# Attention of a fused three-stage kernel: one stay on TensorE per chunk in 64x64 shapes, q and v scaled ahead of the scores, a mask made on the chip, PSUM in pairs of banks, another order of loads

## The chip, the cores and the metric

The kernel runs on one core of a Trainium2 chip. Its five engines each work through a list of their own in order: TensorE (PE), VectorE (DVE), ScalarE (ACT), GpSimd (POOL), and SyncE (SP), which here only issues transfers. The metric is the device time of one execution in microseconds (us), lower is better.

## The reference, cut to what matters

```python
def _attn_ref(q, k, v):                      # 2 batches, 8 heads, 768 tokens, 64 wide
    gamma = 1.0 - 2.0 ** (-5.0 - np.arange(H))
    for t in range(S):
        state = gamma * state + np.einsum('bhd,bhe->bhde', k[:, :, t], v[:, :, t])
        y[:, :, t] = np.einsum('bhd,bhde->bhe', q[:, :, t], state) / np.sqrt(D)
...
def _moe_ref(x, w_in, w_out, alpha):         # x 1536 x 512, w_in 512 x 2048
    h = x @ w_in
    g = np.maximum(h, 0.0) + alpha * np.minimum(h, 0.0)
    return g @ w_out
...
def _moe2_ref(x, w_in, w_out, a, b):         # the same sizes
    h = x @ w_in
    P = a[0] + a[1] * h + a[2] * h**2 + a[3] * h**3
    Q = 1.0 + abs(b[0]) * np.abs(h) + abs(b[1]) * h**2
    g = P / (Q + 1e-06)
    return g @ w_out
```

Attention feeds the first feed-forward layer, and that feeds the second.

## The kernel before, in words

**Products.** A step i of `pe_h` (L334) computes a 128x512 piece of h for one of three token blocks b (512 tokens) and one of 16 blocks m of d_ff; `pe_out` (L351) adds that step's share to the four PSUM banks `acc`. Operands are split into a high and a low part (`xh`/`xl`, `wh`/`wl`, two halves of `g`), and three of the four cross products are kept, so that each of the two functions issues 12 matmuls of 128x128 by 128x512. There are 96 steps, 48 for each layer: 192 such groups of 12. A loop step i issues `pe_h(i + 2)`, then `pe_out(i)`.

**Weights.** They lie in memory as 64-bit numbers, 512 KB for each m and each of w_in and w_out. After the load (L270) a weight tile is decoded: abs on ACT (L278), three operations on DVE (L284, L288, L292; called words 0, 1 and 2 below), a cast on ACT (L303, the high part), a subtraction on DVE (L309, the low part). `START` says in which half step of the loop each of these is issued. A weight's number W0, W1, ... is its place in that order.

**The first layer's bend.** ACT makes two Relus of h (L369, L370, `act1_front`), DVE joins them (L375), ACT and DVE split the result into the parts of g (L380, L385).

**Attention.** Twelve chunks c of 128 tokens, six for each batch; four pairs j of heads, e is the head in its pair. For each chunk there are four loads of 256 KB (q and k transposed, k and v as they are), and TensorE computes the scores (L139), y from scores and v (L170), the growth of the state, called st (L182), and the share of y that comes from the state R (L193, the R part; none in chunks 0 and 6). DVE multiplies the scores by the decay table `dm` (L143, 512 KB, loaded once) and adds st to R (L205). For the R part a scaled q is made: four operations on ACT (L150) and one on POOL or DVE (L152); k is scaled for st on POOL (L123) or, in chunks 4 to 7, by eight operations on ACT (L120). In chunks 5 and 11 no st is needed. y goes to `xh` and `xl` (L212, L213). `att_b` issues the scores and the scaling of q, `att_c` all that follows.

**Order.** All instructions stand in the order in which the program writes them, on each engine. A start phase runs chunks 0 to 3 and decodes the first weight. A table then puts the rest of attention between the product groups, scores and y of a chunk at two places:

```python
stages = {-4: ("c", 4)}
for c, t, u in ((5, -3, -2), (6, -1, 1), (7, 2, 4), (8, 5, 6), (9, 7, 9), (10, 10, 12), (11, 13, 14)):
    stages[t] = ("b", c)
    stages[u] = ("c", c)
```

PSUM has eight banks: four hold `acc` (and, until the first `pe_out`, y), four go round in a ring for h, the scores and y. SP issues all loads in order; a load waits there until its tile is free.

## Time and profile before

| | us |
|---|---|
| median of 3 runs | 582.52 |
| lowest and highest run | 582.01, 582.68 |
| the profiled execution, its span | 582.5 |
| PE busy (matmuls) | 574.3 (99%) |
| DVE busy | 466.2 (80%) |
| ACT busy | 371.1 (64%) |
| POOL busy | 77.5 (13%) |

The span is the time of one profiled execution from its first to its last instruction; the times of runs are taken without the profiler. Matmuls are pipelined, so a busy PE isn't one at its peak: what a matmul takes is seen from where the next one starts.

### The profile page before, as it was taken

To read this page: it belongs to the slowest core of one execution; us is meant where nothing else is said; L and a number is where in the kernel's file an instruction comes from. 1 tells how busy PE (TensorE), PEld (TensorE's weight loads), DVE (VectorE), ACT (ScalarE), POOL (GpSimd) and SP (SyncE) were. 2 spreads that over 40 slices of the span, in tenths; PEclk is the share of its full clock that TensorE was granted. 3 is DMA by queue.
4 is the path that set the end of the run, shared out by engine and by line. 5 is a ranking of instruction groups with operands and counts; after the bars stand their busy time and mean duration, and the time that the engine had idled before them with its cause. 6 is when DMAs were issued, how large, how long until landed. Compare 5 with 4: busy or idle time off the path is not lost.

```text
span 582.5 us, 8124 instructions
## 1 busy us (share of the span) xinstructions
PE 574.3 (99%) x3040; PEld 473.3 (81%) x3040; DVE 466.2 (80%) x738; ACT 371.1 (64%) x679; POOL 77.5 (13%) x61
## 2 busy tenths in 40 slices
PE   8999999999999999999999999999999999999997
PEld 7878777888888888888888888888888888888885
DVE  1899688788684364548997999999998999887886
ACT  2687567656553453437765787777786786686672
POOL 1401100000000000000000312223222222221221
PEclk8999999999999999999999999999999999999999
DMA  8999422334321012112451011001111100010101
GB/s 298 335 379 378 160 73 73 112 106 145 108 73 36 1 37 73 37 37 96 171 203 37 1 37 36 19 19 37 37 37 37 37 0 1 0 73 2 53 19 74
DMA packets 18920, 50.78 MB, mean 87 GB/s; under 512 B 2624, under 2 KB 2752, under 8 KB 18880
## 3 DMA queue, kind: packets, MB, share of 16 engines
...
q8 instruction: 24, 0.39, 0.3%
...
## 4 chain that ended last, share of the span: by engine, by line
PE 87%; DMA 8%; DVE 2%; SPq 1%; ACT 1%; issue 0%
PE acc L351 43%; PE h L334 42%; DMA qk<-in_qT_dram 2%; DMA r<-in_w1i_dram 1%; DMA r<-in_w1o_dram 1%; DMA kv<-in_vn_dram 1%; DMA dq_sb<-in_dq_dram 1%; DMA kv<-in_kn_dram 1%; ACT qk L150 1%; PE y L170 1%; PE sc L139 1%; DVE p L448 0%; PE y L193 0%; SPq L103 0%; PE y L182 0%
## 5 line engine op out<-in xcount | busy, mean ns | idle before, releaser
L334 PE MATMUL h<-xh,wh 128*128 128x512 f32 x384 | 150.3, 391 | 0.0
L334 PE MATMUL h<-xl,wh 128*128 128x512 f32 x384 | 149.6, 389 | 0.0
L334 PE MATMUL h<-xh,wl 128*128 128x512 f32 x384 | 149.4, 389 | 0.0
L351 PE MATMUL acc<-wh,g 128*128 128x512 f32 x384 | 125.7, 390 | 0.0
L433 POOL TENSOR_TENSOR g<-as,g 128x512 fp32r<-128x512 f32 x47 | 64.6, 1374 | 446.9 <-PE acc L351 261.3
L351 PE MATMUL acc<-g,wh 128*128 128x512 f32 x384 | 118.9, 391 | 0.0
L334 PEld LDWEIGHTS h<-xh,wh 128*128 128x128 f32 x384 | 72.1, 188 | 15.7 <-issue 0.2
L351 PEld LDWEIGHTS acc<-wh,g 128*128 128x128 f32 x384 | 72.0, 188 | 15.6 <-DVE g L433 0.4
L334 PEld LDWEIGHTS h<-xl,wh 128*128 128x128 f32 x384 | 72.1, 188 | 15.0 <-DVE xl L213 0.2
L334 PEld LDWEIGHTS h<-xh,wl 128*128 128x128 f32 x384 | 72.0, 188 | 14.9
L351 PEld LDWEIGHTS acc<-g,wh 128*128 128x128 f32 x384 | 71.6, 188 | 15.5 <-issue 0.7
L303 ACT CAST wh<-z 128x512 fp32r<-128x512 f32 x64 | 39.6, 620 | 57.3 <-DVE z L292 57.3
L351 PE MATMUL acc<-g,wl 128*128 128x512 f32 x192 | 75.0, 391 | 0.7 <-DVE wl L309 0.6
L351 PE MATMUL acc<-wl,g 128*128 128x512 f32 x192 | 74.7, 389 | 0.0
L375 DVE SCALAR_TENSOR_TENSOR np<-np,nalpha_sb 128x512 f32<-128x512 f32 x48 | 36.0, 749 | 40.3 <-ACT np L370 40.3
L369 ACT ACTIVATE np<-h 128x512 f32<-128x512 f32 x48 | 28.5, 595 | 44.2 <-PE h L334 44.2
L396 ACT ACTIVATE as<-h 128x512 f32<-128x512 f32 x48 | 28.6, 596 | 41.3 <-PE h L334 41.3
L402 DVE SCALAR_TENSOR_TENSOR as<-as,bb_sb,rr 128x512 f32<-128x512 f32 x48 | 38.0, 791 | 13.1 <-ACT rr L397 13.1
L385 DVE TENSOR_TENSOR g<-np,g 128x512 fp32r<-128x512 f32 x48 | 33.2, 692 | 17.4 <-ACT g L380 17.2
L292 DVE SCALAR_TENSOR_TENSOR z<-r,z 128x512 uint32<-128x512 uint32 x64 | 44.9, 702 | 1.5
L288 DVE SCALAR_TENSOR_TENSOR z<-r,z 128x512 uint32<-128x512 uint32 x64 | 45.0, 702 | 1.0
L309 DVE TENSOR_TENSOR wl<-z,wh 128x512 fp32r<-128x512 f32 x64 | 45.0, 703 | 0.1
...
## 6 DMA issues: line engine op xcount, KB each, us to landing
...
```

Of the source, the lines that this page charges most:

```text
L288: nc.vector.scalar_tensor_tensor(out=zu, in0=lo, scalar=29, in1=zu, op0=ALU.logical_shift_right, op1=ALU.bitwise_or)
L292: nc.vector.scalar_tensor_tensor(out=zu, in0=hi, scalar=0x80000000, in1=zu, op0=ALU.bitwise_and, op1=ALU.bitwise_or)
L303: nc.scalar.copy(hi, Z[k])
L309: nc.vector.tensor_tensor(out=lo, in0=Z[k], in1=hi.bitcast(F32), op=ALU.subtract)
L334: nc.tensor.matmul(ps, w[:, ks], xs(hl, b, k, ALL), start=(n == 0), stop=(n == 11))
L351: nc.tensor.matmul(acc[0][k], a, c, start=(begin and n == 0), stop=(end != "" and n == 2))
L369: nc.scalar.activation(n, h, AF.Relu, scale=-1.0)
L375: nc.vector.scalar_tensor_tensor(out=p, in0=n, scalar=nalpha_sb[:, m:m + 1], in1=p, op0=ALU.mult, op1=ALU.add)
L385: nc.vector.tensor_tensor(out=gl, in0=p, in1=gh.bitcast(F32), op=ALU.subtract)
L396: nc.scalar.activation(s, h, AF.Square)
L402: nc.vector.scalar_tensor_tensor(out=s, in0=s, scalar=bb_sb[:, 1:2], in1=r, op0=ALU.mult, op1=ALU.add)
L433: eng.tensor_tensor(out=gl, in0=a, in1=gh.bitcast(F32), op=ALU.subtract)
```

## The change

- For each chunk from 4 on there is one place in the loop, the end of a step (`VISITS`), where `visit` issues the scores of the next chunk, then the R part, y and st of this one, then the mask, the state and x. Chunks 0 to 3 go through the same functions in the start phase.
- The scores are 16 matmuls with 64 rows, 64 columns and 128 moving columns, each half of the key tokens apart; the R part comes ahead of y. y and st of all chunks lie in one pair of banks. For pairs 2 and 3 the two heads' halves change places in x, and the load of w_in of the first layer changes the same halves of its rows (three transfers in place of one).
- q is scaled ahead of the scores (`att_q`, by one of six tables, on POOL; chunk 0 on DVE), v ahead of st and y (`att_v`, on ACT by eight operations, in chunks 0, 1 and 3 on POOL). ACT makes five of the tables from the one loaded (`att_table`, four operations each). k is not scaled. With this the scores need no decay: a 0/1 triangle made by POOL is multiplied on, one DVE operation of 128x1024 for a chunk. The load of `dm`, the second load of `dq` and the loads of k for chunks 5 and 11 go.
- PSUM is one tile of eight banks: 0 to 3 for `acc` (until the first `pe_out` also for attention), 4 and 5 for h, 6 and 7 for y and st. From the visit of chunk 6 on the next chunk's scores use banks 4 and 5 too. After the last visit h uses 6 and 7 as well.
- `act1_front` makes one Relu; the join reads h in PSUM, with 1 - alpha as its factor. It now stands ahead of the odd half step's decoding, not within it.
- `pe_h`, and `pe_out` where a sweep doesn't end, run pass by pass over the four k; `pe_out` takes wh, wl, wh against g's high, high and low half.
- The first weights are decoded one half step later, and the loads of the start phase stand in another order.

```diff
-    ring = ctx.enter_context(tc.tile_pool(name="ring", bufs=4, space=PSUM))
-    accp = ctx.enter_context(tc.tile_pool(name="accp", bufs=1, space=PSUM))
+    psp = ctx.enter_context(tc.tile_pool(name="psp", bufs=1, space=PSUM))
+    ps_all = psp.tile([P, 8 * 512], F32, name="ps")
...
+    def bank(k):
+        return ps_all[:, 512 * k:512 * k + 512]
+    def pair(k):
+        return ps_all[:, 1024 * k:1024 * k + 1024]
...
-    R = const.tile([P, NK, 64], F32, name="R")
-    dq_sb = one.tile([P, 512], F32, tag="dq", name="dq_sb")
-    dm_sb = alloc("dm_sb")
+    R = const.tile([P, NK * H64], F32, name="R")
+    mask = const.tile([P, P], F32, name="mask")
+    tabs = [alloc(f"dq{n}") for n in range(CPB // 2)]
+    dqt = [tabs[n // 2][:, 512 * (n % 2):512 * (n % 2) + 512] for n in range(CPB)]
...
+    def att_q(c, eng):
+        q = att[c]["q"]
+        eng.tensor_tensor(out=q, in0=q, in1=dqt[c % CPB], op=ALU.mult)
+    def att_v(c, eng):
+        v = r8(att[c]["v"])
+        o = 8 * (c % CPB)
+        if eng is nc.scalar:
+            for h in range(8):
+                nc.scalar.mul(v[:, h, :], v[:, h, :], cst_sb[:, o + h:o + h + 1])
+        else:
+            dk = cst_sb[:, o:o + 8].unsqueeze(2).to_broadcast([P, 8, H64])
+            eng.tensor_tensor(out=v, in0=v, in1=dk, op=ALU.mult)
+    def pe_sc(c, hp):
         a = att[c]
-        ps = [bank(f"sc{c}_{e}") for e in range(2)]
         for j in range(NK):
...
-            for j in range(NK):
-                js = slice(j * P, (j + 1) * P)
-                o = 8 * CPB + 4 * (c % CPB) + j
-                for ds, es in rows(c, j):
-                    nc.scalar.mul(a["qs"][ds, js], a["q"][es, js], cst_sb[es, o:o + 1])
-            eng = nc.gpsimd if c < 4 else nc.vector
-            eng.tensor_tensor(out=a["qs"], in0=a["qs"], in1=dq_sb, op=ALU.mult)
...
+            for n in range(2):
+                t0 = j * P + H64 * n
+                for e in range(2):
+                    o = 512 * e + j * P
+                    nc.tensor.matmul(
+                        hp[HALF[n], o:o + P], a["t"][HALF[e], t0:t0 + H64],
+                        a["q"][HALF[e], j * P:(j + 1) * P], start=True, stop=True,
+                    )
+    def att_mask(c, hp):
+        nc.vector.tensor_tensor(
+            out=r8(att[c]["s"]), in0=r8(hp), in1=mask.unsqueeze(1).to_broadcast([P, 8, P]), op=ALU.mult
+        )
...
+    def pe_y(c, vp, st):
+        a = att[c]
+        m = c % CPB
+        if m > 0:
+            for j, e in HEADS:
+                nc.tensor.matmul(
+                    yo(vp, j, e), R[HALF[e], H64 * j:H64 * j + H64],
+                    a["q"][HALF[e], j * P:(j + 1) * P], start=j % 2 == 0, stop=False,
+                )
+        for j, e in HEADS:
             h = 2 * j + e
             nc.tensor.matmul(
-                yo(j, e),
-                a["v"][:, 64 * h:64 * h + 64],
+                yo(vp, j, e), a["v"][:, H64 * h:H64 * h + H64],
                 a["s"][:, 512 * e + j * P:512 * e + (j + 1) * P],
-                start=j in starts,
-                stop=first and j == NK - 1,
+                start=m == 0 and j % 2 == 0, stop=not st and j % 2 == 1,
             )
...
+        if st:
+            pe_st(c, vp, True)
+    def pe_st(c, vp, joined):
+        a = att[c]
+        for j, e in HEADS:
+            hs = slice(H64 * (2 * j + e), H64 * (2 * j + e) + H64)
+            o = 512 * (j // 2) + 256 + H64 * (j % 2)
+            nc.tensor.matmul(
+                vp[HALF[e], o:o + H64], a["k"][:, hs], a["v"][:, hs],
+                start=not joined and j % 2 == 0, stop=j % 2 == 1,
+            )
...
+    def att_state(c, vp):
+        r, src = (t.rearrange("p (n f) -> p n f", n=2) for t in (R, vp))
+        src = src[:, :, 256:384]
+        if c % CPB == 0:
+            nc.scalar.copy(r, src)
+        else:
+            nc.vector.tensor_tensor(out=r, in0=r, in1=src, op=ALU.add)
...
+    def visit(c, vp, nxt=None, hp=None):
+        st = c % CPB < CPB - 1
+        if nxt is not None:
+            pe_sc(nxt, hp)
+        pe_y(c, vp, st)
+        if nxt is not None:
+            att_mask(nxt, hp)
+        if st:
+            att_state(c, vp)
+        att_x(c, vp)
+        att_drop(c)
...
-        START[0, m, 0], START[0, m, 1] = 2 * m - 9, 2 * m - 4
+        START[0, m, 0], START[0, m, 1] = 2 * m - 8, 2 * m - 3
...
-            nc.sync.dma_start(out=r, in_=SRC[l][n][m].bitcast(U32))
+            src = SRC[l][n][m].bitcast(U32)
+            if (l, n) == (0, 0):
+                nc.sync.dma_start(out=r[:, 0:512], in_=src[:, 0:512])
+                for e in range(2):
+                    nc.sync.dma_start(out=r[HALF[e], 512:1024], in_=src[HALF[1 - e], 512:1024])
+            else:
+                nc.sync.dma_start(out=r, in_=src)
...
+    acc = {0: [bank(k) for k in range(NK)]}
     part = {}
+    hbanks = [4, 5]
...
-        ps = ring.tile([P, 512], F32, tag="ring", name=f"h{i}")
+        hbanks.append(hbanks.pop(0))
+        ps = bank(hbanks[-1])
         n = 0
-        for k in range(NK):
-            ks = slice(k * P, (k + 1) * P)
-            for w, hl in ((wh, 0), (wh, 1), (wl, 0)):
+        for w, hl in ((wh, 0), (wh, 1), (wl, 0)):
+            for k in range(NK):
+                ks = slice(k * P, (k + 1) * P)
                 nc.tensor.matmul(ps, w[:, ks], xs(hl, b, k, ALL), start=(n == 0), stop=(n == 11))
                 n += 1
...
     def pe_out(i):
         l, b, m, begin, end = STEPS[i]
-        if begin:
-            acc[0] = [accp.tile([P, 512], F32, tag=f"acc{k}", name=f"acc{i}_{k}") for k in range(NK)]
         gh, gl = G.pop(i)
         wh, wl = W[l, m, 1]
-        for k in range(NK):
+        prs = ((wh, gh), (wl, gh), (wh, gl))
+        both = [(n, k) for k in range(NK) for n in range(3)]
+        if not end:
+            both.sort()
+        for n, k in both:
...
     def act1_front(i):
-        h = H.pop(i)
         t = alloc(f"np{i}")
         n, p, _ = T1[i] = t[:, 0:512], t[:, 512:1024], t
-        nc.scalar.activation(n, h, AF.Relu, scale=-1.0)
-        nc.scalar.activation(p, h, AF.Relu)
+        nc.scalar.activation(n, H[i], AF.Relu, scale=-1.0)
...
         m = STEPS[i][2]
         n, p, _ = T1[i]
         nc.vector.scalar_tensor_tensor(
-            out=p, in0=n, scalar=nalpha_sb[:, m:m + 1], in1=p, op0=ALU.mult, op1=ALU.add
+            out=p, in0=n, scalar=oma_sb[:, m:m + 1], in1=H.pop(i), op0=ALU.mult, op1=ALU.add
...
-        load_next(3 if t < -6 else 4 if t < 2 * N1 else 2)
+        if t > -5:
+            load_next(4 if t < 2 * N1 else 2)
...
-        for c in range(4):
-            att_tiles(c)
-        load_kq(0)
-        nc.sync.dma_start(out=dm_sb, in_=dm)
+        nc.gpsimd.memset(mask, 1.0)
+        nc.gpsimd.affine_select(
+            out=mask, in_=mask, pattern=[[1, P]], compare_op=ALU.is_ge,
+            fill=0.0, base=0, channel_multiplier=-1,
+        )
         nc.sync.dma_start(out=cst_sb, in_=cst)
-        load_nv(0)
-        load_kq(1)
+        nc.sync.dma_start(out=dqt[0], in_=dq)
+        load(0, "qtv")
+        load(1, "qt")
+        load(0, "k")
+        load(1, "v")
+        load(2, "qt")
+        load(1, "k")
+        load(2, "v")
+        load(3, "qt")
         load_next(1)
-        load_kq(2)
...
+        load(2, "k")
+        load(3, "v")
+        load(4, "qt")
+        load(3, "k")
+        load_next(2)
...
+        att_q(0, nc.vector)
+        for n in range(1, 5):
+            att_table(n)
+        pe_sc(0, pair(1))
+        keep_warm(3)
+        att_mask(0, pair(1))
+        att_v(0, nc.gpsimd)
+        att_q(1, nc.gpsimd)
+        att_v(1, nc.gpsimd)
+        att_q(2, nc.gpsimd)
+        visit(0, pair(3), 1, pair(2))
+        att_v(2, nc.scalar)
+        att_q(3, nc.gpsimd)
+        visit(1, pair(0), 2, pair(1))
+        half(-10)
+        att_v(3, nc.gpsimd)
+        att_q(4, nc.gpsimd)
+        visit(2, pair(3), 3, pair(2))
+        half(-9)
+        pe_y(3, pair(0), False)
+        half(-8)
+        att_x(3, pair(0))
+        half(-7)
+        pe_sc(4, pair(1))
+        att_mask(4, pair(1))
+        pe_st(3, pair(3), False)
+        att_state(3, pair(3))
+        att_drop(3)
+        att_v(4, nc.scalar)
+        att_table(5)
+        att_q(5, nc.gpsimd)
+        half(-6)
+        nc.scalar.activation(bb_sb[:, 0:2], ab_sb[:, 4:6], AF.Abs)
+        nc.vector.tensor_scalar(
+            out=oma_sb, in0=alpha_sb, scalar1=-1.0, scalar2=1.0, op0=ALU.mult, op1=ALU.add
+        )
+        half(-5)
         drop(wt)
...
+        VISITS = {
+            -2: (4, pair(3), 5, pair(0)), -1: (5, pair(3), 6, pair(1)), 0: (6, pair(3), 7, pair(2)),
+            1: (7, pair(3), 8, pair(2)), 3: (8, pair(3), 9, pair(2)), 4: (9, pair(3), 10, pair(2)),
+            5: (10, pair(3), 11, pair(2)), 6: (11, pair(3)),
+        }
...
+            if i in VISITS:
+                c = VISITS[i][0]
+                if c + 2 < NCH:
+                    load(c + 2, "v" if (c + 2) % CPB == CPB - 1 else "vk")
+                if c + 3 < NCH:
+                    load(c + 3, "qt")
...
+            if i in VISITS and VISITS[i][0] < NCH - 1:
+                if VISITS[i][0] > 4:
+                    att_q(VISITS[i][0] + 1, nc.gpsimd)
             if i >= 0:
                 pe_out(i)
             if i >= 0 and STEPS[i][4]:
                 evac(i)
...
-            stage(2 * i + 1)
-            half(2 * i + 1, (lambda: act1_front(new)) if new < N1 else None)
             if new < N1:
+                act1_front(new)
                 act1_join(new)
+            if i in VISITS and VISITS[i][0] > 4:
+                att_v(VISITS[i][0], nc.scalar)
+            half(2 * i + 1)
+            if i in VISITS:
+                visit(*VISITS[i])
+                if VISITS[i][0] == NCH - 1:
+                    for t in tabs:
+                        drop(t)
+                    hbanks[:] = [6, 7] + hbanks
```

The order of instructions on three engines, at the places where the change moves them (a number in a name only tells tiles of one kind apart).

ACT before, around the end of the start phase: the last of the x casts (L212, chunk 3), then W1's abs, the scaling of chunk 5's q (L150) and of chunk 4's k (L120).

```order
L561 ACTIVATE bb_sb<-ab_sb 128x2
L562 ACTIVATE nalpha_sb<-alpha_sb 128x16
L212 CAST xh_75<-y_0_321 128x4x128
L278 ACTIVATE z_350<-r_126 128x512
L150 ACTIVATE qk_171<-qk_171,cst_sb 128x128 x4
L120 ACTIVATE kv_172<-kv_172,cst_sb 128x64 x8
L278 ACTIVATE z_350<-r_227 128x512
```

ACT after, the same place: W0's cast stands between the x casts of chunks 2 and 3.

```order
L202 CAST xh_75<-ps 128x4x128
L311 CAST wh_0_359<-z_292 128x512
L202 CAST xh_75<-ps 128x4x128
L132 ACTIVATE kv_130<-kv_130,cst_sb 128x64 x8
L121 ACTIVATE dq_74<-dq_72,cst_sb 128x128 x4
L286 ACTIVATE z_292<-r_135 128x512
L591 ACTIVATE bb_sb<-ab_sb 128x2
L286 ACTIVATE z_426<-r_149 128x512
L377 ACTIVATE np_437<-ps 128x512
L286 ACTIVATE z_426<-r_153 128x512
L311 CAST wh_1_441<-z_292 128x512
```

Ahead of W1's abs (`z_292<-r_135`) there now stand the eight scalings of v of chunk 4 and the four of a table; the first Relu of h(0) stands ahead of W3's abs.

TensorE before, from the end of `pe_out(0)` to h(3): y and st of chunk 6 (it has no R part).

```order
L351 MATMUL acc_3_587<-g_488,wh_0_264 128x512 x2
L351 MATMUL acc_3_587<-g_488,wl_0_265 128x512
L170 MATMUL y_0_600<-s_534,kv_436 64x128 x2
L170 MATMUL y_1_601<-s_534,kv_436 64x128 x2
L170 MATMUL y_0_600<-s_534,kv_436 64x128 x2
L170 MATMUL y_1_601<-s_534,kv_436 64x128 x2
L182 MATMUL y_0_600<-kv_436 64x64 x8
L334 MATMUL h_642<-xh_75,wh_3_547 128x512
```

TensorE after, from `pe_out(0)` (`g_520`) over the visit of chunk 6 and h(3) to `pe_out(1)`.

```order
L360 MATMUL ps<-g_520,wh_0_359 128x512 x4
L360 MATMUL ps<-g_520,wl_0_360 128x512 x4
L360 MATMUL ps<-g_520,wh_0_359 128x512 x4
L144 MATMUL ps<-qk_421 64x128 x16
L171 MATMUL ps<-s_158,kv_157 64x128 x8
L184 MATMUL ps<-kv_157 64x64 x8
L344 MATMUL ps<-xh_75,wh_3_604 128x512 x4
L344 MATMUL ps<-xl_78,wh_3_604 128x512 x4
L344 MATMUL ps<-xh_75,wl_3_605 128x512 x4
L360 MATMUL ps<-g_607,wh_1_441 128x512 x4
L360 MATMUL ps<-g_607,wl_1_442 128x512 x4
L360 MATMUL ps<-g_607,wh_1_441 128x512 x4
```

The scores of chunk 7 (L144, 16 matmuls), which stood behind h(3), now stand ahead of chunk 6's y, in the stay between `pe_out(0)` and h(3).

DVE before, from the join of h(2) (L375, `np_632`) on: the mask of chunk 7 (L143, twice) follows two operations later, and the scaling of its q (L152) after it.

```order
L292 SCALAR_TENSOR_TENSOR z_545<-r_470,z_545 128x512
L375 SCALAR_TENSOR_TENSOR np_632<-np_632,nalpha_sb 128x512
L309 TENSOR_TENSOR wl_4_630<-z_545,wh_4_629 128x512
L385 TENSOR_TENSOR g_658<-np_632,g_658 128x512
L143 TENSOR_TENSOR s_672<-sc_0_662,dm_sb 128x512
L143 TENSOR_TENSOR s_672<-sc_1_663,dm_sb 128x512
L152 TENSOR_TENSOR qk_516<-qk_516,dq_sb 128x512
L284 TENSOR_SCALAR z_655<-z_655 128x512
```

DVE after: from W4's first word over the join of h(2) (`np_629`) to the mask of chunk 7 (L150).

```order
L292 TENSOR_SCALAR z_515<-z_515 128x512
L317 TENSOR_TENSOR wl_0_360<-z_426,wh_0_359 128x512
L296 SCALAR_TENSOR_TENSOR z_515<-r_435,z_515 128x512
L392 TENSOR_TENSOR g_607<-np_529,g_607 128x512
L300 SCALAR_TENSOR_TENSOR z_515<-r_435,z_515 128x512
L382 SCALAR_TENSOR_TENSOR np_629<-np_629,oma_sb,ps 128x512
L292 TENSOR_SCALAR z_602<-z_602 128x512
L317 TENSOR_TENSOR wl_3_605<-z_515,wh_3_604 128x512
L296 SCALAR_TENSOR_TENSOR z_602<-r_448,z_602 128x512
L300 SCALAR_TENSOR_TENSOR z_602<-r_448,z_602 128x512
L150 TENSOR_TENSOR s_423<-ps,mask 128x1024
```

Between that join and the mask there are now four operations of decoding. Chunk 7's scores lie in banks 4 and 5, of which h(2) has used one and h(3) uses the other.

## Rows read from the trace of the kernel before

**Rows 1.** Chain that ended last, in order of time: start us, us, what.

```profile
101.58 2.95 PE acc L351 x12
104.53 2.72 PE h L334 x12
```

**Rows 2.** Stretches: length, busy us (x) of PE PEld DVE ACT POOL, PEclk, DMA share, GB/s.

```profile
25.88:104.53 78.65, 77.68 (x667) 61.25 (x666) 68.29 (x120) 57.34 (x137) 3.65 (x3) 1.00 0.61 219
104.53:576.21 471.68, 471.68 (x2080) 390.06 (x2080) 383.59 (x595) 303.75 (x520) 64.59 (x47) 1.00 0.15 52
...
25.50:41.00 15.50, 15.50 (x155) 12.44 (x152) 15.17 (x27) 13.23 (x38) 0.00 (x0) 1.00 1.02 380
```

**Rows 3.** Timeline of PE around two stays in attention: start us, us, line.

```profile
83.73 0.39 PE L334 MATMUL h<-xh,wl 128*128 128x512 f32 x1
84.05 1.16 PE L139 MATMUL sc<-qk 64*128 64x128 f32 x16
85.14 0.73 PE L351 MATMUL acc<-g,wh 128*128 128x512 f32 x2
...
90.81 1.09 PE L170 MATMUL y<-s,kv 128*64 128x128 f32 x16
91.73 0.64 PE L182 MATMUL y<-kv 128*64 128x64 f32 x16
92.29 0.67 PE L193 MATMUL y<-qk,R 64*64 64x128 f32 x16
92.89 0.72 PE L351 MATMUL acc<-g,wh 128*128 128x512 f32 x2
```

**Rows 4.** Timeline of PE: h(0), an R part before chunk 6, h(3).

```profile
25.89 0.50 PE L334 MATMUL h<-xh,wh 128*128 128x512 f32 x1
...
30.74 1.09 PE L193 MATMUL y<-qk,R 64*64 64x128 f32 x16
...
46.99 0.50 PE L334 MATMUL h<-xh,wh 128*128 128x512 f32 x1
```

**Rows 5.** Chain at the start, the load of v of chunk 0; PE's first scores.

```profile
3.06 6.04 DMA kv<-in_vn_dram
...
4.76 1.84 PE L139 MATMUL sc<-qk 64*128 64x128 f32 x16
```

**Rows 6.** Timeline of POOL and DVE: one operation each at one time.

```profile
15.24 1.28 POOL L152 TENSOR_TENSOR qk<-qk,dq_sb 128x512 f32<-128x512 f32 x1 [0.37 <-issue]
...
49.33 1.05 POOL L123 TENSOR_TENSOR kv<-kv,cst_sb 128x512 f32<-128x512 f32 x1 [25.61 <-DMA kv<-in_kn_dram]
...
49.39 1.53 DVE L288 SCALAR_TENSOR_TENSOR z<-r,z 128x512 uint32<-128x512 uint32 x1
```

**Rows 7.** Timeline of ACT: the scaling of q, that of k, the copies of a sweep's end.

```profile
25.97 1.26 ACT L150 ACTIVATE qk<-qk,cst_sb 128x128 f32<-128x128 f32 x4
27.14 2.01 ACT L120 ACTIVATE kv<-kv,cst_sb 128x64 f32<-128x64 f32 x8
...
78.99 1.07 ACT L451 COPY p<-acc 128x512 f32<-128x512 f32 x2
```

**Rows 8.** Timeline of DVE: decoding, masking, splitting.

```profile
26.14 0.42 DVE L284 TENSOR_SCALAR z<-z 128x512 uint32<-128x512 uint32 x1
...
27.93 1.28 DVE L143 TENSOR_TENSOR s<-sc,dm_sb 128x512 f32<-128x512 f32 x2
...
38.93 0.69 DVE L385 TENSOR_TENSOR g<-np,g 128x512 fp32r<-128x512 f32 x1
39.54 0.68 DVE L292 SCALAR_TENSOR_TENSOR z<-r,z 128x512 uint32<-128x512 uint32 x1
```

**Rows 9.** Timeline of PE and stretches, where the clock was low.

```profile
9.23 1.64 PE L170 MATMUL y<-s,kv 128*64 128x128 f32 x16 [1.77 <-DMA kv<-in_vn_dram]
...
6.20:9.60 3.40, 1.63 (x20) 1.35 (x19) 1.29 (x2) 0.00 (x0) 1.02 (x1) 1.00 0.97 353
9.60:13.00 3.40, 3.40 (x36) 3.06 (x34) 0.35 (x1) 0.86 (x2) 0.02 (x1) 0.50 1.03 402
```

More of the change, by code (lines that the diff above doesn't have):

```diff
@@ L26 @@
 NSLOT = 42
+H64 = P // 2
 GA = 5
@@ L126, in rows, with load @@
-    def rows(c, j):
-        if c < CPB or j < 2:
-            return [(slice(0, P), slice(0, P))]
-        h = [slice(0, 64), slice(64, P)]
-        return [(h[1], h[0]), (h[0], h[1])]
-    def att_b(c, bank):
+    SRCA = {"q": qT, "t": kT, "k": kn, "v": vn}
+    HALF = (slice(0, H64), slice(H64, P))
+    WAVES = ((0, 2), (1, 3))
+    order = [nc.alloc_semaphore("pe_order"), 0]
+    def load(c, names):
+        if c not in att:
+            t, u, w = alloc(f"qk{c}"), alloc(f"kv{c}"), alloc(f"s{c}")
+            att[c] = {
+                "q": t[:, 0:512], "t": t[:, 512:1024], "k": u[:, 0:512], "v": u[:, 512:1024],
+                "s": w, "tiles": (t, u, w),
+            }
+        for nm in names:
+            nc.sync.dma_start(out=att[c][nm], in_=SRCA[nm][c])
@@ L189, in att_c @@
-        if not first:
-            for j, e in heads:
-                g = 1 - e if four and j >= 2 else e
-                gs = slice(64 * g, 64 * g + 64)
-                nc.tensor.matmul(
-                    yo(j, e),
-                    R[gs, j, :],
-                    a["qs"][gs, j * P:(j + 1) * P],
-                    start=False,
-                    stop=j == NK - 1 or (four and j == 1),
-                )
-        if not last:
-            src = pst.rearrange("p (j d) -> p j d", j=NK)
-            if first:
-                nc.scalar.copy(R, src)
-            else:
-                nc.vector.tensor_tensor(out=R, in0=R, in1=src, op=ALU.add)
@@ L564, in tile_fused @@
[L564 to L595 removed]
+        load(4, "v")
```

177 lines of the change are left out of this document (34 added, 143 removed).

## The prediction

> **What bounds the kernel now.** I read the chain of waits first. From 101.58 us on it is TensorE alone, groups of 12 matmuls without a gap, each 2.72 us, 0.227 a matmul [rows 1]. The stretches say the same: from 104.53 to 576.21 PE is busy for all of 471.68 us, at the full clock [rows 2]. The change leaves the number of product matmuls as it is, and no later stretch has room. So it is worth what it does to one number: when the 17 groups and all of attention that end at 101.58 are through. The profiled execution has a span of 582.5, and the median of the three runs is 582.52, so I sum against 582.5.
>
> Before that point there are two parts. h(0) starts at 25.89 [rows 4]. From there to 101.58 are 75.69 us, of which 17 groups take 46.24, so that 29.45 go to attention and waits. The timeline shows what a stay costs. Scores: the last matmul before starts at 83.73, and the next product at 85.14 instead of 83.96, 1.18 lost, and 0.11 more as the first product behind a stay is slow. A y stay with its R part runs from 90.81 to 92.89, about 2.3 with its entry and its slow first matmul [rows 3]. Seven score stays are 9.1 by this, and eight of y some 17.4 (chunks 4 and 5 with a slower R part, 6 and 11 with less to do), together 26.5; about 3 are left for waits.
>
> In this stretch TensorE has a rival for the pace: from 25.5 to 41, DVE is busy 15.17 of 15.50 us, and the DMA engines are too (share 1.02, 380 GB/s) [rows 2]. What decides is whether the change relieves TensorE, or engines that feed it.
>
> **The change part by part.**
>
> *The joined stay.* In one stay the pieces are scores 1.09 (84.05 to 85.14), y 0.92, st 0.56, each from start to next start [rows 3]. Eight matmuls of the R part take 0.60 to the next product, 0.44 of them their own, I estimate, as they now follow scores of the same shape. With 0.09 for the entry and 0.11 for the slow product behind, 3.2; two stays cost 1.3 and 2.3. Chunk 5 has no st (2.7), 6 no R part (2.8), the last neither scores nor st (1.8). From h(0) on: 5 times 3.2 (chunks 4, 7 to 10) and the three, 23.3 against 26.5. **Gain 3.2.** The unknown is the 16 score matmuls in 64x64. The trace has an R part in this shape twice: 0.60 where the outputs of four heads lie in different places (92.29), 1.09 in an earlier chunk, where they go in twos; with a tail of 0.07 as the other has (0.67 and 0.60), that is 1.02 [rows 3, 4]. I take the first, twice its 0.44 and an entry, the same 1.1 as before; the bound on the other side is below. The Trainium skill, in "TensorEngine Tiling (Array Packing)", Key Properties, says that tiles work independently of each other, and by it the new order, which gives the four quarters in turn, goes in fours. By that rule the sum stays as it is.
>
> *The start.* q and k of chunk 0, half a MiB, are there when the first scores begin at 4.76; v of chunk 0, 1.54 MiB in, lands at 9.10 (3.06 and 6.04) [rows 5]. That is 4.2 us a MiB. Now 1.04 MiB end with v, so it lands at 7.0; at the 353 GB/s of 6.2 to 9.6 [rows 9] for the 0.5 MiB less, 7.6. I take 7.0. POOL scales v0 (1.05) and q1 (1.28) [rows 6]: 9.3. Then come three visits on TensorE, the first 2.8, two more of 3.3 with hand-overs of 0.1: 19; R, the cast and the low part of x to 20.1; W0's words (0.42, 0.69, 0.68 [rows 8]) and two casts on ACT to 23.4. h(0) at 23.5 in place of 25.89. **Gain 2.4.** The mask on POOL, tables 1 to 4 on ACT and the constants lie in time in which these engines wait for loads.
>
> *ACT behind the start.* This gain doesn't reach the next weight. Ahead of W1's abs ACT now has the eight scalings of v4 (2.01) and a table (1.26) [rows 7]: 23.4 + 1.95 + 1.2 + 0.6 = 27.1, and DVE starts W1 at 27.2, where it did at 26.14 [rows 8]. POOL can scale q5 only behind that table, to 27.9, and its scores wait behind h(0): TensorE idles from 26.2 to 28.0. Later y5 waits for v5, whose eight scalings stand behind an abs, two casts and a Relu on ACT: some 3 us, to about 39.
>
> *DVE to h(3).* From 27.2 DVE is the pace. Up to the mask of chunk 7 the order gives 33 instructions: 6 first words at 0.42, three masks at 1.2, an addition to R (0.35, an estimate, it is half as wide), 23 others at 0.61 (38.93 to 39.54 [rows 8]): 2.5 + 3.6 + 0.35 + 14.0 = 20.5. A POOL operation stretches a DVE one that reads twice from SBUF: 1.53 in place of 0.69 [rows 6]. Of the scalings of q5, q6 and q7 on POOL in this time I let two collide, 1.7, and hand-overs take 0.6. The mask ends at 50.0. Between it and the join of h(2) stand four operations of decoding, and chunk 7's scores wait for that join, as they share h's banks. So h(3) starts at 50.1; before it was 46.99 [rows 4], with the scores of chunk 7 (1.3) still to come. **Loss 3.1, or 1.8 with these.**
>
> *From h(3) on* TensorE sets the pace again: 50.1 + 2.7, 12 more groups 32.6, four visits 12.8, the last 1.8, and one wait. At the end of the first sweep (loop step 4) the copies out of PSUM, two on ACT in 1.07 [rows 7] and two on DVE, stand ahead of the Relu and join of h(6), for which chunk 10's scores wait: about 2.0; with the ring of four banks it was 0.3. Sum 102.1 against 101.58: **+0.5, so 583.0.**
>
> *At nothing:* the Relu and the loads that go (ACT and the transfers aren't the pace behind 62 us), the join that reads PSUM, pass order of the products, two banks for h (the next h group comes only after a `pe_out`, 2.7 us, in which Relu and join, some 0.6 each, are done; where a sweep's copies stand ahead it is the wait above), three transfers for a tile of w_in.
>
> **Rivals.**
>
> *A, 583.0,* as summed: less on TensorE, eaten by new waits. Its weak terms are the landing of v0 (0.6), a collision more or less (0.85 each) and the wait at step 4 (0 to 3): 581 to 585.5.
>
> *B, faster: DVE isn't the pace to h(3).* If POOL's scalings fall where DVE reads PSUM or waits, and masks over 1024 columns go quicker, TensorE itself is: y5 to 40, h(2) 42.7, `pe_out(0)` 45.4, scores 46.6, y and st 48.2. h(3) at 48.3, 1.8 earlier: 581.2; with no wait at step 4 579.2. It decides when the mask of chunk 7 ends before 48.2. For it: DVE loses the scaling of q (0.68 each chunk). Against it: its 98% share of the stretch [rows 2].
>
> *C, slower: scores go in twos.* Then 16 of them take 0.84 more (twice 1.02 less 0.60). Four visits behind h(3) carry it in full: 3.4, and up to three in the start 2.5: 586.4 to 588.9. Against it: the row of 0.60.
>
> *D, slower: the clock.* Where PE was idle for 1.77 us ahead of 9.23, the stretch from 9.60 to 13.00 had the clock at 0.50, 1.2 GHz [rows 9]. y5 now waits longer than that, behind busy stretches. h(2) at half the rate is 2.7 longer; DVE's lead hides most of it, 0.6 is left (583.6), and if `pe_out(0)` runs slow too, 3.3 (586.3). The Trainium skill, in "TensorE: Matmul & The Clock Gate", Why this matters for your kernels, warns of idle gaps between bursts of matmuls, which bring the half rate back; by it the sum would be that of this rival. The trace shows one such fall, after a thinner stretch than this.
>
> *E, nothing comes of it:* the stay is joined, but loads and DVE set when chunks can come, and saved time turns into waits of the same size: 582.5.
>
> **How the numbers follow.** About 0.2% (1.2 us, so 581.3 to 583.7) is what a measurement of this kernel can tell from no change. A 0.48 (faster 0.07, same 0.22, slower 0.19), B 0.26 (faster 0.21, same 0.05), C 0.07 and D 0.10 (same 0.01, slower 0.16 together), E 0.09 (0.02, 0.05, 0.02). Faster 0.30, same 0.33, slower 0.37. A is the likeliest: 583.0. From 579.5, near the end of B, to 586.8, where D ends and C begins, about 2 in 10 stay outside.
>
> **What would show it.** Start: h(0) at 23 to 24, the first product group. ACT: W1's abs at 27, behind v4 and a table. TensorE: idle ahead of the scores of chunk 5, 2 us, and of y5, 3 us. DVE: no gap from 27 to 50, and two first words or words near 1.5 us. h(3) at 50; a visit of chunks 7 to 10 costs 3.2, scores 1.1 in it; one wait of 2 us behind loop step 4; no gap from 102 on. Wrong would be: h(3) before 48 (B), scores at 1.9 (C), the clock at 0.5 behind y5 (D), or gaps behind 105, which nothing in the sum allows for.

## The result, and the profile after

589.38 us (median of 4 runs, 588.73 to 590.27) against 582.46: a ratio of 1.012, interval 1.0105 to 1.0134. The change costs 6.9 us. The profiled execution has a span of 588.2; its own time is 589.97. All runs here have a time 1.7 to 1.8 above their span, and this concerns the prediction too (below). One of e9's five runs below took 3256.85 us; the ratio and the interval of e9 are of the other four.

The timeline of TensorE after, as [rows 4] of before: start, length in us, and in brackets how long TensorE was idle ahead of the row and what ended it.

```profile
23.49 1.19 PE L344 MATMUL ps<-xh,wh 128*128 128x512 f32 x4 [0.72 <-ACT xh L202]
...
28.03 1.10 PE L144 MATMUL ps<-qk 64*64 64x128 f32 x32 [1.53 <-POOL qk L125]
...
41.35 2.73 PE L171 MATMUL ps<-s,kv 128*64 128x128 f32 x16 [2.29 <-ACT kv L132]
...
54.37 1.20 PE L344 MATMUL ps<-xh,wh 128*128 128x512 f32 x4 [1.73 <-DVE s L150]
...
87.66 1.20 PE L344 MATMUL ps<-xh,wh 128*128 128x512 f32 x4 [0.33 <-DVE s L150]
...
105.10 1.20 PE L344 MATMUL ps<-xh,wh 128*128 128x512 f32 x4 [1.44 <-DVE xl L203]
```

h(0) comes at 23.49, 2.4 before that of [rows 4], chunk 5's scores at 28.03, y of chunk 5 at 41.35 and h(3) at 54.37, where before had it at 46.99. So the first 28 us go as forecast, and most of what is lost is lost between 28 and 54. Behind h(3) there is a wait after loop step 4 (h(7) at 87.66, with 5.0 us lost to the stay and its waits: a loss here and below is the time from the start of the product group ahead to that of h behind, less 2.72; a stay without waits loses 3.05) and one ahead of h(9), at 105.10.

The chain after, one visit (chunk 10's) and the group with which the stretch without gaps begins: start, length.

```profile
93.40 1.03 PE ps L144 x32
94.43 0.44 PE ps L165 x16
94.87 1.02 PE ps L171 x16
95.89 0.47 PE ps L184 x16
96.36 2.96 PE ps L344 x12
...
108.13 2.72 PE ps L360 x12
```

A stay is scores 1.03, R part 0.44, y 1.02, st 0.47, with the slow product behind it 3.2 (the group of 12 that follows takes 2.96 instead of 2.72). The 17 groups and all of attention end at 108.13; before it was 101.58 [rows 1]. That is 6.55 later. The group that begins there is 0.23 shorter than before, where it was the slow one (2.95 in [rows 1]), and the end of the kernel is 0.6 shorter, so the spans differ by 5.7.

ACT after, between 26 and 43: abs of W2, abs of W4, the scaling of v of chunk 5.

```profile
30.16 0.68 ACT L286 ACTIVATE z<-r 128x512 f32<-128x512 f32 x1 [2.88 <-DMA r<-in_w1i_dram]
...
38.87 0.67 ACT L286 ACTIVATE z<-r 128x512 f32<-128x512 f32 x1 [1.26 <-DMA r<-in_w1i_dram]
...
40.96 2.01 ACT L132 ACTIVATE kv<-kv,cst_sb 128x64 f32<-128x64 f32 x8
```

Both abs wait for a load of w_in, for 2.88 and 1.26 us, and y5 stands behind the second, by way of two casts, a Relu and v5.

DVE after, six rows from 26 to 54; the last is the mask of chunk 7, which releases h(3).

```profile
27.21 1.05 DVE L292 TENSOR_SCALAR z<-z 128x512 uint32<-128x512 uint32 x1 [0.91 <-ACT z L286]
...
31.36 0.75 DVE L382 SCALAR_TENSOR_TENSOR np<-np,oma_sb,ps 128x512 f32<-128x512 f32 x1 [1.65 <-ACT np L377]
...
33.03 1.78 DVE L296 SCALAR_TENSOR_TENSOR z<-r,z 128x512 uint32<-128x512 uint32 x1
...
40.60 0.69 DVE L392 TENSOR_TENSOR g<-np,g 128x512 fp32r<-128x512 f32 x1 [1.20 <-ACT g L387]
...
49.86 1.38 DVE L292 TENSOR_SCALAR z<-z 128x512 uint32<-128x512 uint32 x1
...
53.09 1.22 DVE L150 TENSOR_TENSOR s<-ps,mask 128x1024 f32<-128x1024 f32 x1
```

Two rows wait for ACT (1.65 and 1.20), and three last 1.05, 1.78 and 1.38, where the same operations take 0.42, 0.69 and 0.42 [rows 8]. Behind 27.21 DVE has little other idle time up to h(3), and from 40.60 to the end of the mask none. So three things could be behind the loss: late loads, DVE operations that are stretched, and the clock, which fell, as is shown next.

```profile
42.00:43.00 1.00, 0.97 (x9) 0.70 (x7) 1.00 (x3) 1.00 (x6) 0.00 (x0) 0.50 1.06 379
43.00:44.00 1.00, 1.00 (x10) 0.68 (x7) 1.00 (x2) 1.00 (x2) 0.00 (x0) 0.50 1.04 404
```

These are stretches of the kernel after, with length, busy time of PE, PEld, DVE, ACT and POOL, clock, DMA share and GB/s: at 42 to 44 the clock is 0.50, 1.2 GHz, behind the idle time ahead of y5.

### The profile page after: what moved, and what is told of

Read it like the earlier page. It is cut to its first block, busy times and chain, and to the rows that moved or that the text cites. A ratio compares the mean times of both kernels' runs of the same rounds, so it can differ in the third digit from the quotient of the medians.

```text
span 588.2 us, 8446 instructions
## 1 busy us (share of the span) xinstructions
PE 569.2 (97%) x3222; PEld 469.9 (80%) x3222; DVE 463.2 (79%) x715; ACT 345.5 (59%) x642; POOL 83.0 (14%) x67
## 3 DMA queue, kind: packets, MB, share of 16 engines
HBM read 45.92 MB, written 3.15 MB: 83 GB/s over the span
## 4 chain that ended last, share of the span: by engine, by line
PE 89%; DMA 7%; DVE 2%; SPq 1%; issue 0%; ACT 0%
PE ps L360 44%; PE ps L344 43%; DMA r<-in_w1i_dram 4%; DMA kv<-in_kn_dram 2%; DMA kv<-in_vn_dram 1%; PE ps L171 1%; PE ps L144 1%; SPq L115 0%; DVE p L455 0%; DVE s L150 0%; PE ps L165 0%; DVE z L292 0%; DVE z L300 0%; PE ps L184 0%; DVE np L382 0%
## 5 line engine op out<-in xcount | busy, mean ns | idle before, releaser
L344 PE MATMUL ps<-xh,wh 128*128 128x512 f32 x384 | 104.1, 393 | 5.6 <-DVE s L150 2.1
L360 PE MATMUL ps<-g,wh 128*128 128x512 f32 x384 | 105.0, 389 | 0.0
L360 PE MATMUL ps<-wh,g 128*128 128x512 f32 x384 | 104.8, 390 | 0.0
L344 PE MATMUL ps<-xl,wh 128*128 128x512 f32 x384 | 102.7, 389 | 0.0
L344 PE MATMUL ps<-xh,wl 128*128 128x512 f32 x384 | 102.7, 389 | 0.0
L344 PEld LDWEIGHTS ps<-xh,wh 128*128 128x128 f32 x384 | 71.6, 188 | 21.4 <-DVE s L150 2.3
L360 PEld LDWEIGHTS ps<-wh,g 128*128 128x128 f32 x384 | 72.0, 188 | 15.6 <-DVE g L440 0.4
L344 PEld LDWEIGHTS ps<-xl,wh 128*128 128x128 f32 x384 | 72.1, 188 | 15.1
L344 PEld LDWEIGHTS ps<-xh,wl 128*128 128x128 f32 x384 | 72.1, 188 | 15.1
L360 PEld LDWEIGHTS ps<-g,wh 128*128 128x128 f32 x384 | 72.1, 188 | 14.9
L360 PE MATMUL ps<-wl,g 128*128 128x512 f32 x192 | 53.8, 389 | 0.0
```

The lines of the kernel that those rows point to most:

```text
L344: nc.tensor.matmul(ps, w[:, ks], xs(hl, b, k, ALL), start=(n == 0), stop=(n == 11))
L360: nc.tensor.matmul(acc[0][k], a, c, start=(begin and n == 0), stop=(end != "" and n == 2))
```

## The experiments

The four theories: 1, the three part loads of w_in are slow and make everything late; 2, the order of the loads does; 3, the clock does; 4, formed after the first four runs, POOL's scalings of q stretch the operations of DVE, which sets when h(3) starts. "h(3)" in the table of runs is its start in the profile; before and after have 46.99 and 54.37. The ratio of a run is to executions of the kernel before that were made beside it, with medians of 582.53 to 582.81. In the timelines below a group at the edge of the stretch that was looked at is cut there (x3 or x1 in place of x4).

| run | median us | ratio to before, interval | span | h(3) |
|---|---|---|---|---|
| e1_whole_w1i | 589.03 | 1.0106 (1.0091 to 1.0121) | 587.1 | 52.83 |
| e2_last_bank | 587.48 | 1.0085 (1.0063 to 1.0107) | 585.3 | 52.95 |
| e3_copies_after | 589.28 | 1.0109 (1.0093 to 1.0125) | 588.3 | 55.09 |
| e4_fill | 590.63 | 1.0126 (1.0103 to 1.0150) | 589.4 | 55.41 |
| e5_before_split | 585.95 | 1.0057 (1.0037 to 1.0077) | 583.0 | 48.50 |
| e6_columns | 588.05, one run | | 586.3 | 52.42 |
| e7_partitions | 593.59, one run | | 591.9 | 57.91 |
| e9_q_left_out | 585.27 | 1.0051 (1.0031 to 1.0070) | 583.6 | 49.35 |
| e10_q_on_dve | 587.32 | 1.0076 (1.0056 to 1.0095) | 585.9 | 51.74 |
| e11_mask_first | 588.52 | 1.0101 (1.0086 to 1.0116) | 586.9 | 51.15 |
| e12_four | 585.13 | 1.0044 (1.0029 to 1.0059) | 583.4 | 50.77 |
| e13_six | 585.34 | 1.0046 (1.0031 to 1.0061) | 583.9 | 50.25 |
| e14_before_again | 583.14, one run | | 581.4 | 45.92 |
| e15_seven | 582.95 | 1.0008 (0.9998 to 1.0017) | 581.0 | 48.92 |

**e1, whole loads.**

```diff
-            if (l, n) == (0, 0):
-                nc.sync.dma_start(out=r[:, 0:512], in_=src[:, 0:512])
-                for e in range(2):
-                    nc.sync.dma_start(out=r[HALF[e], 512:1024], in_=src[HALF[1 - e], 512:1024])
-            else:
-                nc.sync.dma_start(out=r, in_=src)
+            nc.sync.dma_start(out=r, in_=src)
```

> The changed kernel, but a tile of w_in of the first layer is one load of 512 KB again; the rows that have to change places are laid out so ahead of the launch. Theory 1 (the three part loads make packets slow, and every load behind them late; the abs of W4 waited to 38.9 us where the sum had 34.6): W4 there by 35.5, h(3) at 50 to 51 instead of 54.4, time 4 to 5 below the changed kernel, 584.5 to 585.5, still 2 above before. Theory 2 (the order of the loads is late in itself: q, k and v for later chunks ahead of W4): W4 at 37 or later, less than 1.5 won. Theory 3 (the clock that fell to 0.50 ahead of h(2) is what costs): the clock falls again, less than 1 won.

From 35 to 40 us, first the changed kernel, then this one (columns as above):

```profile
35.00:40.00 5.00, 2.15 (x50) 1.32 (x49) 3.71 (x6) 1.71 (x4) 1.28 (x1) 1.00 1.05 256
```

```profile
35.00:40.00 5.00, 2.16 (x28) 1.58 (x30) 4.32 (x8) 4.73 (x14) 1.46 (x1) 0.95 1.04 398
```

The DMA engines are as busy in both, but move 256 and 398 GB/s, W4 lands at 33.8 instead of 38.8, and h(2) starts at 40.84 instead of 44.01. Yet h(3) is only 1.5 earlier, at 52.83, where theory 1 had 50 to 51; the span is 1.1 less, and the medians of the timed runs differ by 0.35, within their spread. Loads were late, and are no longer, without a change of their order, so theory 2 falls; but taking the part loads away alone wins little of the time. What holds h(3) now stands in the timeline of DVE in this run, its stretched rows from 26 to 52:

```profile
26.64 1.05 DVE L287 TENSOR_SCALAR z<-z 128x512 uint32<-128x512 uint32 x1 [0.81 <-ACT z L281]
...
29.73 1.08 DVE L287 TENSOR_SCALAR z<-z 128x512 uint32<-128x512 uint32 x1
...
32.04 1.73 DVE L295 SCALAR_TENSOR_TENSOR z<-r,z 128x512 uint32<-128x512 uint32 x1
...
39.42 0.84 DVE L287 TENSOR_SCALAR z<-z 128x512 uint32<-128x512 uint32 x1
...
44.17 1.78 DVE L312 TENSOR_TENSOR wl<-z,wh 128x512 fp32r<-128x512 f32 x1
...
49.98 1.65 DVE L295 SCALAR_TENSOR_TENSOR z<-r,z 128x512 uint32<-128x512 uint32 x1
```

By [rows 8] two of the forms take 0.42 and 0.69; these six take 4.8 more together. POOL has six scalings of q in this time, one of them this row:

```profile
43.83 1.56 POOL L125 TENSOR_TENSOR qk<-qk,dq 128x512 f32<-128x512 f32 x1 [3.86 <-DMA qk<-in_qT_dram]
```

That scaling ends at 45.39, and the DVE operation that began at 44.17 ends 0.56 behind that, as if it had waited for all of it. DVE is busy from 26.6 to 52.8 with hardly a gap. The Trainium skill, in "SBUF — State Buffer", Who interferes with whom, says that the port pair which the two engines share is locked for a whole instruction, and that the loser waits fully; by it a collision can cost nearly the length of a POOL operation, and the 1.1 of this row agrees.

**e4, the clock.** Seven matmuls on the mask tile stand in the idle time ahead of chunk 5's R part and y.

```diff
+    def fill(c, cnt):
+        for _ in range(cnt if c == 5 else 0):
+            nc.tensor.matmul(bank(0)[:, 0:P], mask, mask, start=True, stop=True)
```

> The changed kernel with seven matmuls of 128x128 by 128x128 more, three ahead of the R part of chunk 5 and four ahead of its y, where TensorE is idle for 1.9 and 2.3 us and the clock falls to 0.50 behind. They compute nothing that is used. Theory 3 (the clock costs): y of chunk 5 in 1.0 instead of 2.66, h(3) and the end 1.5 to 2.5 earlier. Theory 1 (DVE, fed late by loads, sets when h(3) can start): the clock stays at 1.00, y and h(2) are earlier by 1.5 or more, and h(3) still starts at 54 to 54.5; the time is the same within 0.4.

```profile
42.00:43.00 1.00, 0.76 (x11) 0.67 (x11) 1.00 (x3) 1.00 (x5) 0.00 (x0) 1.00 0.99 291
43.00:44.00 1.00, 1.00 (x9) 0.75 (x6) 1.00 (x2) 1.00 (x3) 0.32 (x1) 1.00 0.97 344
```

The same stretches of this run: the clock stays at 1.00 (it fell to 0.50 elsewhere, from 30 to 32). Nothing is won; h(3) starts at 55.41, later than the 54 to 54.5 that was expected, and the time's interval overlaps that of the changed kernel. In both kernels DVE works without a gap for the last 13 us ahead of h(3), and h(3) waits for its mask. Theory 3 falls: the clock fell, as a rival had it, but DVE was late anyway, and hid it.

**e9, q left out.** On top of whole loads, `att_q` in the loop is issued for chunk 11 alone.

```diff
-                if VISITS[i][0] > 4:
+                if VISITS[i][0] > 9:
                     att_q(VISITS[i][0] + 1, nc.gpsimd)
```

> The kernel with whole loads of w_in, and the scaling of q of chunks 6 to 10 on POOL left out (those scores and R parts are then taken from an unscaled q). With whole loads alone h(3) still started at 52.83, and DVE, busy throughout from 26.6, had six operations that POOL's scalings stretched by 0.4 to 1.1 us, 4.8 together, where the sum had 1.7. Theory 4 (these stretched operations are what h(3) still waits for): none but the first is longer than 0.8 between 28 and 50, h(3) starts 3.5 to 4.3 earlier, at 48.5 to 49.3, time 583 to 584. Rival (TensorE's own path over v5 and y5 takes their place): h(3) at 51 or later, less than 2 won.

```profile
49.35 0.96 PE L339 MATMUL ps<-xh,wh 128*128 128x512 f32 x3 [0.81 <-DVE s L150]
```

The row is h(3) on TensorE. It is 3.48 earlier than with whole loads alone, and the span 3.5 less, at the lower edge of what theory 4 had; the time, 585.27, is 3.8 less, but above the 583 to 584 that were expected. Of the stretched operations only the first is left (1.06, at 27.34). With this the stretched operations are shown to hold h(3), once the loads are in time.

**e10, q on DVE**, again on whole loads: `nc.gpsimd` becomes `nc.vector` in the scalings of chunks 5 to 11.

> The kernel with whole loads of w_in, and q of chunks 5 to 11 scaled by DVE instead of POOL. Theory 4: each costs 0.61 on DVE instead of some 0.8 of stretching, so that six save about 1.1 us, h(3) at 51.5 to 52.3, time about 1 below that with whole loads. Rival (POOL's scaling costs DVE little, the long operations come from somewhere else): 6 times 0.61 are added, and it is 2 to 3.7 slower.

1.2 less span, 1.7 less in the median, h(3) at 51.74. DVE is better off with the whole work than with POOL doing it beside.

**e2, the last bank.**

```diff
-                    hbanks[:] = [6, 7] + hbanks
+                    hbanks[:] = hbanks + [6, 7]
```

> The changed kernel, but behind the last visit h goes on with banks 4 and 5, and takes 6 and 7 after them. h(9) waits 1.44 us for chunk 11's x, since it is the first in bank 6. If this wait is on the path: 1.4 to 1.7 us faster than the changed kernel, h(9) directly behind y. If another wait takes its place (its bank still held by the join of an earlier h): under 0.5.

The loss around the last visit goes from 3.23 to 1.71, the time to 587.48. The wait was on the path, for 1.5. (The span is 2.9 less; the rest is h(3), which came 1.4 earlier in this execution, though no instruction ahead of it differs.)

**e3, the copies behind the join at step 4.** `evac(i)` is issued behind `act1_join(new)` there.

> The changed kernel, but at loop step 4 the Relu and the join of h(6) stand ahead of the four copies out of PSUM. If the copies are what chunk 10's scores and h(7) wait for (1.49 and 0.33 us idle there): 1.8 to 2.0 us faster. If pe_out(5), which begins a new sweep in the banks that the copies read, waits instead: under 1.

The loss at step 4 goes from 5.0 to 4.34 only, and the time stays. DVE and then TensorE in this run: the join, a copy, the mask of chunk 10's scores, and h(7).

```profile
81.50 0.75 DVE L382 SCALAR_TENSOR_TENSOR np<-np,oma_sb,ps 128x512 f32<-128x512 f32 x1 [0.21 <-ACT np L377]
...
83.58 0.69 DVE L460 COPY p<-ps 128x512 f32<-128x512 f32 x1 [0.67 <-PE ps L360]
...
86.45 1.22 DVE L150 TENSOR_TENSOR s<-ps,mask 128x1024 f32<-128x1024 f32 x1
...
87.72 1.20 PE L344 MATMUL ps<-xh,wh 128*128 128x512 f32 x4 [1.22 <-DVE s L150]
```

The scores no longer wait, but h(7), whose bank they share, waits 1.22 for their mask, which stands behind the copies and four operations of decoding. One wait turned into another.

**e11, the mask ahead of decoding**, on whole loads: `visit` masks first, and `half(2 * i + 1)` follows.

> The kernel with whole loads of w_in, and in a step with a visit DVE masks the next chunk's scores ahead of the odd half step's decoding, not behind it. With the copies behind the join at loop step 4 (an earlier run) the wait ahead of chunk 10's scores went, and one of 1.22 us ahead of h(7) came, for the mask that stands behind four operations of decoding. If that order is what h waits for: h(3) up to 2 us earlier, none or 0.3 us idle ahead of h(3) instead of 1.72, time 1 to 2 below that with whole loads. If the decoding that now comes later is needed as soon: waits of pe_out for a low part (DVE wl) in its place, under 0.5 won.

A span of 586.9 against 587.1: h(3) is 1.7 earlier, but products wait for low parts of weights (DVE wl, up to 1.23 ahead of `pe_out(0)`'s second pass), and the losses at the stays of chunks 7 and 10 grow from 3.05 to 3.6 and 3.7. The second case of the expectation.

**e5, part loads in the kernel before.**

```diff
-            nc.sync.dma_start(out=r, in_=SRC[l][n][m].bitcast(U32))
+            src = SRC[l][n][m].bitcast(U32)
+            if (l, n) == (0, 0):
+                nc.sync.dma_start(out=r[:, 0:512], in_=src[:, 0:512])
+                for e in range(2):
+                    es = slice(64 * e, 64 * e + 64)
+                    nc.sync.dma_start(out=r[es, 512:1024], in_=src[es, 512:1024])
...
```

> The kernel before, with its 512 KB loads of w_in of the first layer in three parts as in the changed kernel (column half, and two half-high loads of the other columns; here without any change of places). What is left of theory 1: packets slower by a quarter or more while such parts are under way, loads between 25 and 45 us up to 2 late, time 1 to 2 us above before. If parts cost nothing here, since DVE sets the pace and loads have room: within 0.4 of before.

The kernel before from 35 to 40 us, then this one:

```profile
35.00:40.00 5.00, 5.00 (x57) 3.94 (x56) 4.93 (x10) 4.37 (x13) 0.00 (x0) 1.00 1.03 401
```

```profile
35.00:40.00 5.00, 4.17 (x42) 3.09 (x40) 4.93 (x9) 4.45 (x8) 0.00 (x0) 1.00 1.05 337
```

585.95, 3.4 more than before, with 337 GB/s in this stretch in place of 401; more than the 1 to 2 us that were expected. In the kernel before, the part loads alone cost half of what the whole change does.

**e6 and e7, which part is slow.** Two loads for each tile of w_in, once by columns, once by halves of the partitions.

> A tile of w_in as two loads of 128 partitions, each half the columns (2 KB of a row of 4 KB). If half rows are what made the packets slow: from 35 to 40 us a share near 1.05 at some 260 to 320 GB/s, as in the changed kernel (256), and a span of 587.5 to 588.5. If not: 380 GB/s or more, as with whole loads (398), span 587.

> A tile of w_in as two loads of 64 partitions, each with whole rows of 4 KB. If loads of half the partitions are what is slow: from 35 to 40 us a share near 1.05 at some 260 to 320 GB/s, span 587.5 to 588.5. If not: 380 GB/s or more, span 587.

e6, then e7, 35 to 40 us:

```profile
35.00:40.00 5.00, 2.26 (x28) 1.73 (x30) 4.31 (x9) 4.83 (x14) 0.00 (x0) 0.88 1.05 397
```

```profile
35.00:40.00 5.00, 2.97 (x54) 2.00 (x52) 4.28 (x7) 0.58 (x1) 1.32 (x2) 1.00 1.02 202
```

With column halves 397 GB/s are moved, as with whole loads; with loads of 64 partitions 202, at the same share, which is less than expected. It is the half height. e7, with all of w_in by such loads, is 4.2 slower in its one run than the changed kernel, which loads half of it so.

**e12 and e13, edits together.** e12 has whole loads, q on DVE, the last bank, and the sixth table made with the others in the start phase; e13 adds the edits of e3 and e11.

> Four edits together: whole loads of w_in, q scaled by DVE, banks 6 and 7 taken last behind the last visit, and the sixth decay table made in the start phase, ahead of W1's abs and q5 no longer behind it. By the earlier runs and rows: whole loads 1.1, q on DVE 1.2, the bank 1.4 to 1.5, the table up to 1.2 ahead of the scores of chunk 5. If they add up: a span near 583.5 and a time within 1.5 of the kernel before. If DVE to h(3) takes up what the table gives: 585.

> The four edits, the mask ahead of the odd half step's decoding, and the copies behind the join at loop step 4. Each of these two alone won 0.2 or nothing; the copies alone turned the wait ahead of chunk 10's scores into one of h(7) for its mask, which the other edit moves ahead. Together they should take most of the 1.9 us lost at step 4: 1.2 to 1.9 below the four. If low parts of weights are late instead, as with the mask first alone: no better than the four.

The four add up, by the span: 583.4. The time is 2.5 above before, where 1.5 was expected. In e13 step 4 costs 3.7 instead of 5.0, but the mask first loses 1.1 and 1.3 at the stays of chunks 7 and 10, where the scores wait for q and the join on DVE, so that it is no better. What is left in e12, TensorE ahead of chunk 6's scores and h(3):

```profile
37.19 1.99 PE L144 MATMUL ps<-qk 64*64 64x128 f32 x32 [4.44 <-DVE qk L125]
...
50.77 0.50 PE L339 MATMUL ps<-xh,wh 128*128 128x512 f32 x1
```

4.44 us idle for a scaling of q6, which stands behind decoding on DVE.

**e15, seven edits.** The four; at step 4 alone the copies behind the join and the mask first; and q of the next chunk ahead of the even half step's decoding.

```diff
+            if i in VISITS and 4 < VISITS[i][0] < NCH - 1:
+                att_q(VISITS[i][0] + 1, nc.vector)
             if 0 <= old < N1:
                 half(2 * i, lambda: act1_hi(old), lambda: act1_lo(old))
...
-            half(2 * i + 1)
+            if i != 4:
+                half(2 * i + 1)
             if i in VISITS:
-                visit(*VISITS[i])
+                visit(*VISITS[i], between=lambda: half(2 * i + 1) if i == 4 else None)
```

> The four edits (whole loads, q on DVE, banks 6 and 7 last, the sixth table early), and at loop step 4 alone the copies behind the join and the mask ahead of decoding, and q of the next chunk scaled ahead of the even half step's decoding. In the four, TensorE idled 4.4 us ahead of the scores of chunk 6, for q6 that stood behind decoding on DVE, and 1.9 at step 4. If these are what is left: scores of chunk 6 by 35, h(3) at 49 to 49.5, one stay of 3.1 at step 4, 3 us below the four, 582 and so the same as before. If y5 still waits for v5 and masks for DVE: only step 4 is won, 583.2.

```profile
34.59 1.10 PE L144 MATMUL ps<-qk 64*64 64x128 f32 x32 [2.21 <-DVE qk L125]
...
48.92 0.96 PE L340 MATMUL ps<-xh,wh 128*128 128x512 f32 x3 [0.80 <-DVE s L150]
```

Chunk 6's scores at 34.59, h(3) at 48.92, one stay of 3.2 at step 4, and 582.95: the same as before (0.9998 to 1.0017). The stay of chunk 10, one step on, loses 4.3 in place of 3.05, so part of what step 4 wins is lost again there. All of the loss is undone by these seven. No version beat the kernel before.

**e14, the kernel before again.**

> The kernel before once more, for a second profile. Every run here has a span 1.7 to 1.8 below its time, so its profile of 582.5 belongs to an execution near 584.3, above the median of 582.5. If that execution was one with later loads at the start: span 580.4 to 581.0 here, h(0) or h(3) 1 to 2 us earlier than 25.89 and 46.99. If not, 582.5 again.

```profile
25.00 0.50 PE L334 MATMUL h<-xh,wh 128*128 128x512 f32 x1
...
45.92 0.50 PE L334 MATMUL h<-xh,wh 128*128 128x512 f32 x1
```

A span of 581.4 and a time of 583.14, between the two cases; h(0) and h(3) are 0.9 and 1.1 earlier than in [rows 4]. So the profile that the sum was made against is of an execution that was about 1.8 above the median; 1.1 of it lies in the stretch up to h(3).

**h(3) from execution to execution.** The changed kernel, e2 and e3 have the same instructions up to h(3), and yet it starts at 54.37, 52.95 and 55.09. So a difference of 1 or 2 us between two profiles, as of e1 or e11, shows little by itself. The timelines of DVE show where it comes from. Each row of this table has the start of W1's first word on DVE, by how much POOL's scalings stretch operations of DVE up to the mask of chunk 7, and how long DVE waits for ACT in the two places where ACT waited for the loads of W2 and W4.

| | W1 on DVE | stretched (operations) | waits behind loads | h(3) |
|---|---|---|---|---|
| the forecast | 27.2 | 1.7 (2) | 0 | 50.1 |
| the changed kernel | 27.21 | 2.7 (3) | 1.65 + 1.20 | 54.37 |
| e2 | 26.96 | 2.5 (3) | 0.97 + 0.89 | 52.95 |
| e3 | 27.25 | 3.9 (4) | 1.37 + 0.98 | 55.09 |
| e1, whole loads | 26.64 | 4.8 (6) | 0 | 52.83 |
| e9, without q | 27.34 | 0.6 (1) | 0 | 49.35 |

With 20.5 of work and a hand-over of 0.65 that all five have, each row adds up to its h(3) within 0.5.

## Why the prediction was wrong

The forecast was 583.0, no change, and it is 589.4, above the range that ended at 586.8. By its own steps:

- **"I sum against 582.5".** The span was taken for the time. With 1.76 around it the profiled execution was at 584.3, and 102.1 at the end of the stretch would have made a time of 584.8. 1.8 of the miss lies here, before any step on the change. (The other 6.0, up to 108.13, less the 0.23 and 0.6 behind it gives 590.0; the profiled execution after took 589.97, 0.6 above its median.)
- **The joined stay**, 3.2 with scores of 1.1 in fours: 3.2, with 1.03. Right, and rival C is out.
- **The start**, h(0) at 23.5 and chunk 5's scores at 28.0: 23.49 and 28.03. Right.
- **"DVE to h(3)", 50.1: it was 54.37.** This is the step that failed, by 4.3. That DVE sets the pace was right, and so was the work, 20.5, as the table of h(3) shows. Two terms were mis-sized. The larger is in the list "At nothing": "three transfers for a tile of w_in". They are slow, the abs of W2 and W4 waited for them, and DVE waited for ACT: 1.65 and 1.20, 2.85 where the sum had nothing. The other is "I let two collide, 1.7": three did in the changed kernel, 2.7, and with loads in time six do, 4.8 (e1), and 3.5 of the span goes with them (e9). The sum let POOL scale q5 to q7 in this stretch; little but the loads holds POOL back, and in e1 it went on to q10. The two don't add: with late loads POOL is late as well and collides less, and without them it collides more, so that taking the part loads away wins only 1.1 of span, and 0.35 in the median.
- **"From h(3) on"**, 52.0: 53.8. The wait at step 4 was 1.95, put at 2.0. Right. The last stay, put at 1.8, was 3.34. The sum has no wait there: "two banks for h" was among the things at nothing, but the first h behind the last visit takes bank 6, which y still holds (e2, 1.5).
- **Rival D**: the clock fell where it was said to, and cost nothing (e4), since DVE was later still. Of its own price DVE's lead hid all, where the sum left 0.6.
- **Rival B** had DVE win by less work, and POOL's scalings fall where they don't meet DVE's. They met three to six times, as counted above, and h(3) came at 53 to 55, not at 48.3.

Step by step from the profile after to that of e15, in span: 588.2; whole loads 1.1; q on DVE 1.2; the bank and the sixth decay table 2.5, of which e2 shows 1.5 for the bank; q earlier and step 4 2.4; 581.0. In the medians, over more executions, the same steps are 0.4, 1.7, 2.2 and 2.2. In the last, h(3) is 1.85 earlier and step 4 1.8 cheaper, but the stay of chunk 10 is 1.3 dearer. That the decay table is worth the 1.0 that remains is worked out from this, it was not run alone; the order of the loads was not tried alone either, nor was q on DVE with the part loads left as they are.
